# Second-quarter weights loaded in halves, block-diagonal states copied in two steps, one product split between two engines: a fused attention and maxout kernel on one core

## The chip, the cores and the metric

The kernel runs on one core of a Trainium2 chip. The metric is the time of one execution on the device in microseconds (us), and the figure used is the median of several executions. One execution was also recorded by the hardware profiler. Its *span* runs from the first to the last recorded instruction; its own time is longer, because launch and completion lie around the span.

The engines are named as in the profile: PE (TensorE matrix multiplies), PEld (its weight loads), DVE (VectorE), ACT (ScalarE), POOL (GpSimd) and SP (SyncE, here the queue that issues nearly all DMAs).

## The reference

Two stages are fused. The first is an attention between a sequence `x` (8 batches, 8 heads, 512 rows, 64 columns) and a small `state` (32 rows per head). It goes both ways: the sequence reads the state and the state reads the sequence. The second is a maxout layer over the 512 joined head columns.

```python
scores = scale * np.matmul(x, state.transpose(0, 1, 3, 2))
a = np.exp(scores - scores.max(-1, keepdims=True))
a /= a.sum(-1, keepdims=True) + 1e-09
xread = np.matmul(a, state)
...
sread = np.matmul(a2, x)            # the same with the roles exchanged
y = np.concatenate([xread, sread], axis=2)
x = y.transpose(0, 2, 1, 3).reshape(B * S, H * D)   # 4352 rows of 512
h1 = x @ w1                          # w1, w2: 512 x 1024
h2 = x @ w2
g = np.maximum(h1, h2)
out = g @ w_out                      # w_out: 1024 x 512
```

## The kernel before, in words

The maximum is written as `max(h1, h2) = relu(h1 - h2) + h2`. So the kernel needs `wd = w1 - w2` (512 x 1024) for the relu branch and `wwo = w2 @ w_out` (512 x 512) for the linear branch. It makes both on the chip, in bf16, from weights that arrive in four quarters of 256 columns of the 1024 (`FQ = 256`, `q` = 0 to 3). Per quarter there are three tensors: `w2f[q]`, `w1f[q]`, `wof[q]`, 512 KB each in f32. `w2_cast` makes the bf16 copy `w2b`, `w2_tr_mm`/`w2_tr_ev` transpose it on PE and copy it to `w2t`, `w_sub` subtracts to `wd`, `wo_cast` makes the bf16 `wo`, and `w_wo_mm` multiplies `w2t` by `wo` (L559; two matmuls for each of the four row blocks `i`, one for each half `f` of the quarter). `w_wo_ev` adds the rounds up in `w2acc`.

For each batch `b` the attention weights `a` (128 rows, four row blocks `c`, two head groups `g`) are transposed into `AT[b]`. The state is multiplied with `wd` and `wwo` beforehand: `sw_mm` makes `SW[b]`. Then `l1_mm` (L433) multiplies `SW[b]` by `AT[b]` for each of eight column blocks `f`, `l1_ev` applies the relu and writes `R[b]`. `l2` (or `l2_open`, L445, and `l2_part`, L449) makes the 512 output columns of one row block in a PSUM bank, and `l2_out` copies them to `OB[b]`, which `store` writes out.

The states stand in the tile `sbd` in block-diagonal form: `sbd[64 j : 64 j + 64, b, k, 32 j : 32 j + 32]`, with `j` = 0, 1. Batches 0 and 1 are brought in by themselves (`load_state`, `state_mm`, `state_ev`). Batches 2 to 7 are loaded together (`load_states`), cast on POOL (`states_cast`), transposed by one DMA into the tile `stt` (`states_dma`, L161), and copied from there into `sbd` by `states_ev(j, eng)`: one copy for each `j`, with 64 partitions and 768 elements.

The order of the work is written out by hand. Each engine runs its instructions in the order of the program text (`manual_schedule`), and waits by semaphores are put in where data or buffers need them. The text has two parts:

* L587 to L855: the loads in order, all weight preparation, the whole of batch 0, and batch 1 up to the end of its first layer. PSUM has two pools of four banks, `ps` and `pa`, handed out in turn. `idle` puts in matmuls on zeros.
* L858 on: the loop over `b` = 1 to 7. For `b` = 1 it begins with the scores and the normalisation of batch 2 (`norm` has its product on POOL) and goes on to batch 1's second layer in four row blocks `c`. After `c` = 1 it puts in `sw_all(2)`.

The loads of SP carry eight semaphores that are used in turn. In the built program the issue of a load therefore waits until the load eight places before it has landed. A load into a buffer that is still read waits for its last reader too: `load_w2(3)` waits for `w_sub(0)` on POOL.

Three places matter for the change. First, the product `norm_mul_pair(0, 2, "P")` at L668 on POOL, behind which POOL has, in this order, `wo_cast_h(0)`, `w1_cast_h(1)`, `wo_cast_h(1)`, `w_sub(0)`, `w2_cast(1)` and `wo_cast(1)` (L716). Next to it DVE has `norm_mul_pair(0, 3, "V")`. Second, L714 to L722, where DVE has `w_sub(1)` and `w2_tr_ev(1)`, and PE then `w_wo_mm(1, 1)`. Third, L829 to L852, where `states_ev(1, "A")` and `states_ev(0, "V")` stand ahead of the eight relu evictions of batch 1 on ACT and DVE; these free the banks that the transposes `sread_tr_mm` (L353) and the scores of batch 2 (L271) take.

Of the kernel before, what the change touches and what calls it, by code (L numbers as in the profile page):

```python
# [8 lines left out]
F32 = mybir.dt.float32  # L9
# [6 lines left out]
def kernel(  # L16
# [9 lines left out]
    nc = tc.nc  # L26
    B, H, S, D = x.shape
    _, _, Ns, _ = state.shape
    L = S + Ns
    DM = H * D  # L30
    FF = moe_w1.shape[1]
    NC = S // 128
    NF = FF // 128
    NQ = 4
    FQ = FF // NQ
# [5 lines left out]
    stage = ctx.enter_context(tc.tile_pool(name="stage", bufs=1))  # L41
# [5 lines left out]
    pa = ctx.enter_context(tc.tile_pool(name="pa", bufs=4, space=bass.MemoryType.PSUM))  # L47
    ctx.enter_context(tc.manual_schedule())

    def bank(dtype=F32, pool=None):  # L50
        n = 512 if dtype == F32 else 1024
        if pool is pa:
            return pa.tile([128, n], dtype, tag="acc", name="acc")
        return ps.tile([128, n], dtype, tag="ps", name="ps")

    def copy(eng, o, i):
        if eng == "A":
            nc.scalar.copy(o, i)  # L58
        elif eng == "V":
            nc.vector.tensor_copy(o, i)  # L60
        else:
            nc.gpsimd.tensor_copy(o, i)  # L62
# [5 lines left out]
    sbd = consts.tile([128, B, 4, 2 * Ns], BF16, name="sbd")  # L68
    wd = consts.tile([128, 4, FF], BF16, name="wd")
    wwo = consts.tile([128, 4, DM], BF16, name="wwo")  # L70
    wo = consts.tile([128, NF, DM], BF16, name="wo")
# [11 lines left out]
    xf_t, st = {}, {}  # L83
# [12 lines left out]
    w2f, w1f, wof, w2b = {}, {}, {}, {}  # L96

    def load_w2(q, second=False):
        wf, w, tag = (w1f, moe_w1, "w1f") if second else (w2f, moe_w2, "w2f")
        wf[q] = stage.tile([128, 4, FQ], F32, tag=tag, bufs=3, name=tag)  # L100
        nc.sync.dma_start(out=wf[q], in_=w[:, q * FQ:(q + 1) * FQ].rearrange("(i p) f -> p i f", p=128))

    def load_w1(q):
        load_w2(q, True)

    def load_wo(q):
        wof[q] = stage.tile([128, 2, DM], F32, tag="wof", bufs=3, name="wof")
        nc.sync.dma_start(out=wof[q], in_=moe_w_out[q * FQ:(q + 1) * FQ, :].rearrange("(f p) n -> p f n", p=128))
# [15 lines left out]
    P = {}  # L124
# [35 lines left out]
        P["st"] = xio.tile([128, NC * 256], BF16, tag="xb", name="stt")  # L160
        nc.sync.dma_start_transpose(out=P["st"].rearrange("p (m r) -> p m r", m=8), in_=sbr.rearrange("p m j d -> p (m j d)"))  # L161

    def states_ev(j, eng):
        o = sbd[64 * j:64 * j + 64, 2:B, :, 32 * j:32 * j + 32].rearrange("p b k (l m) -> p (b k) l m", l=4)
        copy(eng, o, P["st"][64 * j:64 * j + 64, :].rearrange("p (m k l) -> p k l m", m=8, l=4)[:, 8:])


    def cast_half(b, g, eng):
# [19 lines left out]
    def cast_pair(b, k, eng, m=1):  # L188
        xo = st[b]["xo"]
        for j in range(k, k + m):  # L190
            copy(eng, xo[:, :, j, 2:130].rearrange("p c (i d) -> p i c d", i=2),
                 xf_t[b][:, 2 * j:2 * j + 2, :].rearrange("p i (c d) -> p i c d", c=NC))

    def xt_pair_mm(b, k, pool=None):
        d = st[b]
        if "xt" not in d:
            d["xt"] = at.tile([128, NC, 4, 128], BF16, tag="xt", name="xt")
        p = P["xt", k] = bank(BF16, pool)
        for c in range(NC):
            nc.tensor.transpose(p[:, c * 128:(c + 1) * 128], d["xo"][:, c, k, 2:130], ident)  # L200

    def xt_pair_ev(b, k, eng):
        copy(eng, st[b]["xt"][:, :, k, :], P["xt", k][:, 0:512].rearrange("p (c t) -> p c t", c=NC))

    def att_tiles(b):
        d = st[b]
        d["e"] = at.tile([128, 2, NC, 4, Ns], BF16, tag="e", name="e")
        d["a"] = at.tile([128, 2, NC, 4, Ns], BF16, tag="a", name="a")
        d["es"] = at.tile([128, 2, 2 * NC, 2], F32, tag="es", name="es")
        d["er"] = at.tile([128, 2, 2 * NC, 2], F32, tag="er", name="er")  # L210

    def scores_pair_mm(b, k, pool):
        d = st[b]
        if "e" not in d:
            att_tiles(b)
        p = P["sc", k] = bank(F32, pool)
        for c in range(NC):
            nc.tensor.matmul(p[:, c * 64:c * 64 + 64], d["xt"][:, c, k, :], sbd[:, b, k, :],
                             start=(c == 0), stop=(c == NC - 1))
# [5 lines left out]
    def reduce_pair(b, k):  # L225
        d = st[b]
        nc.vector.tensor_reduce(d["es"][:, k // 2, :, k % 2], d["e"].rearrange("p g c i n -> p (g c) i n")[:, :, k, :],
                                axis=mybir.AxisListType.X, op=ALU.add)
# [65 lines left out]
        (nc.gpsimd if eng == "P" else nc.vector).tensor_mul(  # L294
            av, ev, d["er"][:, hh].unsqueeze(3).to_broadcast([128, 2 * NC, 2, Ns]))

    def norm_mul_pair(b, k, eng):
        d = st[b]
        ev = d["e"].rearrange("p g c i n -> p (g c) i n")[:, :, k, :]
        av = d["a"].rearrange("p g c i n -> p (g c) i n")[:, :, k, :]  # L300
        (nc.gpsimd if eng == "P" else nc.vector).tensor_mul(
            av, ev, d["er"][:, k // 2, :, k % 2].unsqueeze(2).to_broadcast([128, 2 * NC, Ns]))

    def norm(b, hh, eng, sums=True):
        norm_sums(b, hh, sums)
# [137 lines left out]
    def l2_open(b, c, p, start, stop):  # L443
        for g in range(2):
            nc.tensor.matmul(p, AT[b][:, g, c, :], SW[b][:, g, FF:WC], start=(start and g == 0), stop=(stop and g == 1))  # L445

    def l2_f(b, c, p, fs, start, stop):
        for j, f in enumerate(fs):
            nc.tensor.matmul(p, R[b][:, f, c * 128:(c + 1) * 128], wo[:, f, :],  # L449
                             start=(start and j == 0), stop=(stop and j == len(fs) - 1))  # L450

    def l2_out(b, c, p, eng):
        if b not in OB:
            OB[b] = big.tile([128, NC, DM], F32, tag="ob", name="ob")
        copy(eng, OB[b][:, c, :], p)

    def l2(b, c):
        p = bank(F32, pa)
        l2_open(b, c, p, True, False)
        l2_f(b, c, p, range(NF), False, True)  # L460
        l2_out(b, c, p, "A" if c % 2 else "V")
# [59 lines left out]
    def wo_cast_h(j, eng):  # L521
        copy(eng, wo[:, j, :], wof[0][:, j, :])
# [23 lines left out]
    def w_sub(q, i0, i1, eng):  # L546
        (nc.gpsimd if eng == "P" else nc.vector).tensor_sub(  # L547
            wd[:, i0:i1, q * FQ:(q + 1) * FQ], w1f[q][:, i0:i1], w2f[q][:, i0:i1])

    def wo_cast(q, eng):  # L550
        copy(eng, wo[:, 2 * q:2 * q + 2, :], wof[q])

    ROUNDS = [[0], [1], [2], [3]]

    def w_wo_mm(r, i, pool=None):
        p = P["wwo", r, i] = bank(F32, pool)
        fs = [f for q in ROUNDS[r] for f in (2 * q, 2 * q + 1)]
        for f in fs:
# [7 lines left out]
    def w_wo_ev(r, i, eng):  # L566
        if r == 0:
            copy(eng, w2acc[:, i, :], P["wwo", r, i])
        else:
            nc.vector.tensor_tensor(wwo[:, i, :] if r == len(ROUNDS) - 1 else w2acc[:, i, :], P["wwo", r, i],  # L570
                                    w2acc[:, i, :], op=ALU.add)
# [3 lines left out]
    def idle(n, cols=256):  # L575
        if idle_p[0] is None:
            idle_p[0] = bank(F32, pa)
        for j in range(n):
            nc.tensor.matmul(idle_p[0][:, 0:cols], wz[:, 0:128], wz[:, 0:cols], start=True, stop=True)  # L579
# [17 lines left out]
    load_h(1, 0)  # L597
    load_state(1, nc.sync)
    load_w2(1)
    load_w1(1)  # L600
    load_wo(1)
    load_w2(2)
    load_w1(2)
    load_w2(3)
# [31 lines left out]
    scores_pair_mm(0, 0, pa)  # L636
    idle(1)
    cast_pair(0, 3, "V")
    xt_pair_mm(0, 2)
    xt_pair_ev(0, 2, "V")  # L640
    state0_neg("P")
    scores_pair_ev(0, 0)
    reduce_pair(0, 0)
    scores_pair_mm(0, 1, pa)
    scores_pair_ev(0, 1)
    reduce_pair(0, 1)
    w2_cast_h(0, "P")
# [17 lines left out]
    sw_h_mm(0, pa)  # L665
    reduce_pair(0, 3)
    norm_sums(0, 1, False)
    norm_mul_pair(0, 2, "P")  # L668
    norm_mul_pair(0, 3, "V")
    wo_cast_h(0, "P")  # L670
    w1_cast_h(1, "P")
    w2_tr_h_ev(0, "A")
# [38 lines left out]
    sw_ev(1, 0, FQ, 0, "A")  # L711
    l2_part(0, 0)
    w2_tr_mm(1)
    w_sub(1, 0, 4, "V")  # L714
    w2_tr_ev(1, "V")
    wo_cast(1, "P")  # L716
    sw_two_mm(1)
    sw_two_ev(1, 1, "V")
    w_wo_ev(0, 0, "A")
# [106 lines left out]
    l2_open(0, 0, ACC[0], False, True)  # L826
    l2_open(0, 1, ACC[1], False, True)
    l2_out(0, 1, ACC[1], "A")
    states_ev(1, "A")  # L829
    l2_out(0, 0, ACC[0], "V")  # L830
    states_ev(0, "V")
    l1_mm(1, 6, pa)
    cast_half(3, 1, "P")
    l1_ev(1, 6, "A")
# [23 lines left out]
    for b in range(1, B):  # L858
        n = b + 1
        if b + 2 < B:  # L860
            if b > 1:
                cast_x(b + 2, ("P", "P"))
                xt_dma(b + 2)
        for f in range(NF if b > 1 else 0):
            l1(b, f)
        if n < B:
            for hh in range(2):
                scores(n, hh)
            for hh in range(2):
                norm(n, hh, "P")  # L870
            at_dma(n)
            if b + 2 < B:
                cast_xo(b + 2)
            if b + 3 < B:
                load_x(b + 3)
        else:
            moe_sread()
        for c in range(NC):
            if b == B - 1 and c == NC - 1:
                l2_last(b, c)  # L880
            else:
                l2(b, c)
            if n < B:
                if c == 1:
                    sw_all(n)
                    sread_mm(n, pa)
                if c == 2:
                    sread_norm(n)
                if c == 3:
                    sread_tr(n, "A")  # L890
            elif c < NC - 1:
                store(b, c, c + 1)
        if n < B:
            store(b)
# [30 lines left out]
```

## Time and profile before

| what | us |
|---|---|
| median of five executions | 148.01 |
| lowest and highest of the five | 147.92 and 149.12 |
| the profiled execution's own time | 148.33 |
| its span | 146.5 |
| PE busy in the span | 140.0 |
| DVE, ACT, POOL busy in the span | 84.0, 70.2, 59.5 |

The granted TensorE clock was 0.995 of full speed over the span. A busy PE is not a PE at its peak, because matmuls are pipelined and their ends are modelled; but where PE's starts follow each other at their least distance, nothing but PE's own work can shorten the stretch. A matmul of 512 columns takes 0.38 us in the profile, and the next one starts 0.216 us after it (16 of L433 take 3.45 us in the chain of waits). PE has 3.68 us of busy time in the first 5 us and 3.78 us in the next 5. The DMA engines moved between 283 and 375 GB/s from about 3.4 to 34.9 us.

### The profile page before, as it was taken

How to read it: one execution, taken by the hardware profiler on the slowest of the kernel's cores; microseconds unless marked ns; L12 is line 12 of the kernel's file. 1: busy time of each engine (PE TensorE's matmuls, PEld its weight loads, DVE VectorE, ACT ScalarE, POOL GpSimd, SP SyncE). 2: the span in 40 equal slices, each digit the busy share in tenths (PEclk: the TensorE clock that was granted, in tenths of full speed). 3: DMA queues.
4: the chain of work that ended last, by engine and by line, in shares of the span. 5: the costliest groups of instructions: out<-in, count | busy, mean ns of one | idle time of the engine just before them, and what ended most of it. 6: DMA issues, size and time to landing. Idle time of an engine off the chain costs nothing.

```text
span 146.5 us, 3213 instructions
## 1 busy us (share of the span) xinstructions
PE 140.0 (96%) x1300; PEld 69.8 (48%) x1300; DVE 84.0 (57%) x173; ACT 70.2 (48%) x135; POOL 59.5 (41%) x81
## 2 busy tenths in 40 slices
PE   6879999999999999999999999999999999999990
PEld 4455444364544445444544444454445344754460
DVE  3484685879786648464854585376557464621110
ACT  4367757786791546236440735171537145511110
POOL 2359644866946522925291447146500500000000
PEclk9999999999999999999999999999999999999998
DMA  4999999999739999498948784877306032402422
GB/s 117 317 325 351 356 361 363 361 350 197 151 63 323 152 349 291 96 169 321 257 85 258 285 183 76 282 293 144 72 2 286 7 72 107 179 4 72 143 111 104
DMA packets 37695, 29.44 MB, mean 201 GB/s; under 512 B 21296, under 2 KB 34864, under 8 KB 36784
## 3 DMA queue, kind: packets, MB, share of 16 engines
q1 hardware_dynamic: 37408, 29.17, 70.0%
q8 instruction: 10, 0.16, 0.5%
q10 hardware_dynamic: 272, 0.07, 0.2%
q14 instruction: 5, 0.04, 0.1%
HBM read 15.34 MB, written 8.91 MB: 165 GB/s over the span
## 4 chain that ended last, share of the span: by engine, by line
PE 83%; POOL 5%; DMA 4%; ACT 3%; issue 1%; DVE 1%; SPq 1%; POOLq 0%; ACTq 0%
PE acc L449 35%; PE ps L433 16%; PE acc L445 10%; PE ps L559 4%; DMA xf<-in_x_dram 4%; PE ps L368 3%; PE ps L489 2%; PE acc L499 2%; PE ps L271 2%; POOL wd L547 2%; POOL wo L62 2%; PE acc L335 1%; PE acc L473 1%; PE acc L497 1%; ACT r L422 1%
## 5 line engine op out<-in xcount | busy, mean ns | idle before, releaser
L449 PE MATMUL acc<-wo,r 128*128 128x512 bf16 x248 | 59.6, 380 | 0.0
L449 PEld LDWEIGHTS <-r 128*128 128x128 bf16 x248 | 23.8, 98 | 28.8 <-issue 0.6
L58 ACT COPY ob<-acc 128x512 f32<-128x512 f32 (+2 forms) x17 | 9.4, 554 | 49.1 <-PE acc L449 27.7
L433 PE MATMUL ps<-aT,sw 128*128 128x512 bf16 x118 | 27.9, 380 | 0.0
L424 DVE TENSOR_SCALAR r<-ps 128x512 bf16<-128x512 f32 x26 | 18.0, 691 | 14.3 <-PE ps L433 14.2
L294 POOL TENSOR_TENSOR a<-e,er 128x512 bf16<-128x512 bf16 x14 | 14.4, 1048 | 26.0 <-ACT e L276 18.8
L422 ACT ACTIVATE r<-ps 128x512 bf16<-128x512 f32 x33 | 19.6, 602 | 6.1 <-PE ps L433 5.5
L62 POOL CAST xb<-xf 128x1024 bf16<-128x1024 f32 x12 | 13.5, 1128 | 16.9 <-DMA xf<-in_x_dram 16.9
L60 DVE COPY ob<-acc 128x512 f32<-128x512 f32 (+1 forms) x17 | 10.9, 644 | 16.3 <-PE acc L449 14.6
L433 PEld LDWEIGHTS <-sw 128*128 128x128 bf16 x128 | 12.2, 98 | 13.7
L62 POOL CAST xo<-xf 128x512 bf16<-128x512 f32 x28 | 16.1, 615 | 5.4 <-DMA xf<-in_x_dram 5.0
L445 PE MATMUL acc<-sw,aT 128*128 128x512 bf16 x62 | 18.2, 381 | 0.0
L60 DVE CAST sw<-ps 128x512 bf16<-128x512 f32 x15 | 9.8, 686 | 11.0 <-PE ps L368 10.6
L58 ACT CAST sw<-ps 128x512 bf16<-128x512 f32 (+1 forms) x21 | 11.0, 574 | 2.9 <-PE ps L368 1.5
L287 DVE TENSOR_REDUCE es<-e 128x16 f32<-128x512 bf16 x14 | 9.2, 656 | 1.8 <-ACT e L276 1.8
L276 ACT ACTIVATE e<-ps 128x512 bf16<-128x512 f32 x14 | 7.8, 604 | 0.8 <-PE ps L271 0.2
L579 PE MATMUL acc<-wz 128*128 128x256 bf16 x32 | 6.6, 343 | 1.2 <-DVE ones L617 1.2
L445 PEld LDWEIGHTS <-aT 128*128 128x128 bf16 x62 | 5.0, 98 | 4.4
L559 PE MATMUL ps<-wo,w2t 128*128 128x512 bf16 x24 | 6.7, 379 | 0.1
L570 DVE TENSOR_TENSOR w2acc<-ps,w2acc 128x512 f32<-128x512 f32 x8 | 5.2, 687 | 1.8 <-PE ps L559 1.7
L547 POOL TENSOR_TENSOR wd<-w1f,w2f 128x1024 bf16<-128x1024 f32 x2 | 4.7, 2356 | 1.7 <-DMA w1f<-in_moe_w_dram 1.7
L271 PEld LDWEIGHTS <-xt 128*128 128x128 bf16 x112 | 4.3, 98 | 2.1 <-issue 0.5
(109 smaller groups left out, 145.3 us busy)
## 6 DMA issues: line engine op xcount, KB each, us to landing
xf<-in_x_dram SPq DMA_DIRECT2D x14, 512.0 KB, 5.0
out_dram<-ob SPq DMA_DIRECT2D x7, 1024.0 KB, 4.2
w2f<-in_moe_w_dram SPq DMA_DIRECT2D x3, 512.0 KB, 6.8
w1f<-in_moe_w_dram SPq DMA_DIRECT2D x3, 512.0 KB, 8.7
wof<-in_moe_w_out_dram SPq DMA_DIRECT2D x3, 512.0 KB, 8.0
xf<-in_x_dram SPq DMA_DIRECT2D x4, 256.0 KB, 3.9
out_dram<-ob SPq DMA_DIRECT2D x3, 256.0 KB, 2.0
w2f<-in_moe_w_dram SPq DMA_DIRECT2D x2, 256.0 KB, 6.1
```

Of the source, the lines that this page charges most:

```text
L58: nc.scalar.copy(o, i)
L60: nc.vector.tensor_copy(o, i)
L62: nc.gpsimd.tensor_copy(o, i)
L276: nc.scalar.activation(out=ev.rearrange("p (g c) i n -> p g c (i n)", g=2), in_=P["sc", hh].rearrange("p (c g m) -> p g c m", c=NC, g=2), ...
L287: nc.vector.tensor_reduce(d["es"][:, hh], ev, axis=mybir.AxisListType.X, op=ALU.add)
L294: (nc.gpsimd if eng == "P" else nc.vector).tensor_mul(av, ev, d["er"][:, hh].unsqueeze(3).to_broadcast([128, 2 * NC, 2, Ns]))
L422: nc.scalar.activation(out=o, in_=p, func=ACTF.Relu)
L424: nc.vector.tensor_scalar(o, p, scalar1=0.0, scalar2=None, op0=ALU.max)
L433: nc.tensor.matmul(p, SW[b][:, g, f * 128:(f + 1) * 128], AT[b][:, g].rearrange("p c t -> p (c t)"), start=(g == 0), stop=(g == 1))
L445: nc.tensor.matmul(p, AT[b][:, g, c, :], SW[b][:, g, FF:WC], start=(start and g == 0), stop=(stop and g == 1))
L449: nc.tensor.matmul(p, R[b][:, f, c * 128:(c + 1) * 128], wo[:, f, :], start=(start and j == 0), stop=(stop and j == len(fs) - 1))
L559: nc.tensor.matmul(p, w2t[:, f, i, :], wo[:, f, :], start=(f == fs[0]), stop=(f == fs[-1]))
```

## The change

There are four edits. (1) `load_w1(1)` and `load_wo(1)` become two loads of 256 KB each: for W1 by row blocks (two of the four), for Wo by halves `f`. Their use is cut the same way: `w_sub(1)` on DVE in two instructions, `wo_cast(1)` on POOL in two. (2) `states_ev` gets a range of batches. Where it stood it now copies batch 2 alone (64 x 128 instead of 64 x 768 elements, on each of ACT and DVE); batches 3 to 7 (64 x 640) are copied in the loop at `b` = 1 after the first row block of the second layer. (3) The product of pair 2 of batch 0 is cut by head group: POOL makes `g` = 0, and DVE makes `g` = 1 after its own product of pair 3. (4) The scores of pair 1 of batch 0 stand ahead of the transposes of pair 2 on PE.

```diff
+    def load_w1_part(q, g):
+
+        if q not in w1f:
+            w1f[q] = stage.tile([128, 4, FQ], F32, tag="w1f", bufs=3, name="w1f")
+        nc.sync.dma_start(
+            out=w1f[q][:, 2 * g:2 * g + 2],
+            in_=moe_w1[256 * g:256 * g + 256, q * FQ:(q + 1) * FQ].rearrange("(i p) f -> p i f", p=128))
...
+    def load_wo_part(q, j):
+        if q not in wof:
+            wof[q] = stage.tile([128, 2, DM], F32, tag="wof", bufs=3, name="wof")
+        nc.sync.dma_start(out=wof[q][:, j, :], in_=moe_w_out[q * FQ + 128 * j:q * FQ + 128 * j + 128, :])
...
-    def states_ev(j, eng):
-        o = sbd[64 * j:64 * j + 64, 2:B, :, 32 * j:32 * j + 32].rearrange("p b k (l m) -> p (b k) l m", l=4)
-        copy(eng, o, P["st"][64 * j:64 * j + 64, :].rearrange("p (m k l) -> p k l m", m=8, l=4)[:, 8:])
+    def states_ev(j, b0, b1, eng):
+        o = sbd[64 * j:64 * j + 64, b0:b1, :, 32 * j:32 * j + 32].rearrange("p b k (l m) -> p (b k) l m", l=4)
+        copy(eng, o, P["st"][64 * j:64 * j + 64, :].rearrange("p (m k l) -> p k l m", m=8, l=4)[:, 4 * b0:4 * b1])
...
-    def norm_mul_pair(b, k, eng):
+    def norm_mul_pair(b, k, eng, g0=0, g1=2):
...
+    def wo_cast_part(q, j, eng):
+        copy(eng, wo[:, 2 * q + j, :], wof[q][:, j, :])
...
-    load_w1(1)
-    load_wo(1)
+    load_w1_part(1, 0)
+    load_w1_part(1, 1)
+    load_wo_part(1, 0)
+    load_wo_part(1, 1)
...
+    scores_pair_mm(0, 1, pa)
     xt_pair_mm(0, 2)
     xt_pair_ev(0, 2, "V")
     state0_neg("P")
     scores_pair_ev(0, 0)
     reduce_pair(0, 0)
-    scores_pair_mm(0, 1, pa)
...
-    norm_mul_pair(0, 2, "P")
+    norm_mul_pair(0, 2, "P", 0, 1)
     norm_mul_pair(0, 3, "V")
+    norm_mul_pair(0, 2, "V", 1, 2)
...
-    w_sub(1, 0, 4, "V")
+    w_sub(1, 0, 2, "V")
+    w_sub(1, 2, 4, "V")
     w2_tr_ev(1, "V")
-    wo_cast(1, "P")
+    wo_cast_part(1, 0, "P")
+    wo_cast_part(1, 1, "P")
...
-    states_ev(1, "A")
+    states_ev(1, 2, 3, "A")
     l2_out(0, 0, ACC[0], "V")
-    states_ev(0, "V")
+    states_ev(0, 2, 3, "V")
...
             else:
                 l2(b, c)
+            if b == 1 and c == 0:
+                states_ev(1, 3, B, "A")
+                states_ev(0, 3, B, "V")
```

## The prediction

> **What bounds the kernel now.** I read the busy time by stage first, since the share over the span mixes stages. The columns are the stage, its length, then busy time and instructions of PE, PEld, DVE, ACT and POOL, the clock, the DMA share and GB/s.
>
> ```profile
> 15.00:18.86 3.86, 3.69 (x44) 1.64 (x43) 2.78 (x5) 3.09 (x7) 2.43 (x3) 1.00 1.09 354
> 18.86:25.00 6.14, 6.14 (x55) 3.15 (x55) 4.72 (x7) 3.46 (x6) 2.08 (x2) 1.00 1.09 367
> ...
> 36.00:38.60 2.60, 2.60 (x49) 1.50 (x42) 1.57 (x7) 1.75 (x3) 2.54 (x5) 1.00 0.42 89
> 38.60:42.42 3.82, 3.48 (x17) 1.57 (x16) 3.82 (x7) 3.76 (x6) 3.47 (x4) 1.00 0.63 120
> 42.42:47.00 4.58, 4.58 (x36) 2.38 (x36) 3.08 (x8) 1.91 (x4) 1.94 (x2) 1.00 0.88 231
> ```
>
> PE fills its stages from 18.86 on, except 38.60 to 42.42, where DVE and ACT are the full ones. So I took the chain of waits next (start, length, what).
>
> ```profile
> 10.63 0.79 POOL a L301
> 11.42 0.55 POOL wo L62
> ...
> 17.76 1.05 POOL wo L62
> 18.81 0.04 issue
> 18.86 1.02 PE ps L559 x4
> ...
> 38.61 0.58 ACT ob L58
> 39.20 0.01 issue
> 39.21 0.02 ACTq L422
> 39.23 1.55 ACT sbd L58
> 40.78 0.02 issue
> 40.80 1.58 ACT r L422 x3
> 42.38 0.04 issue
> 42.42 0.22 PE acc L353
> ```
>
> It shows three regimes: up to 18.86 POOL's queue sets the pace, from 18.86 to 38.6 and from 42.4 to the end PE's own work does, and between them ACT. From 42.4 on every piece is PE's, so a microsecond won before 42.4 stays won if no later load or buffer is late. The change touches the first and the third regime only. Last I read the timelines around each edit; their rows are named as they are used, and these carry most:
>
> ```profile
> 10.52 0.42 DVE L301 TENSOR_TENSOR a<-e,er 128x256 bf16<-128x256 bf16 x1
> 10.63 0.79 POOL L301 TENSOR_TENSOR a<-e,er 128x256 bf16<-128x256 bf16 x1 [0.25 <-DVE er L288]
> ```
>
> **The states (edit 2), the larger term.** PE starts the first layer of batch 1 at 38.41 and the scores of batch 2 at 42.48: 4.07 us. Its work in between is 16 matmuls at 0.216 (3.45) and two transposes at 0.056 (0.11), together 3.56. The lost 0.51 is one wait: the second transpose at L353 takes the bank that ACT's third relu (L422) frees at 42.38, and that relu is late because ACT's copy of 1.55 stands before all of them. In the change this copy has 128 instead of 768 elements. The nearest rows are ACT's 64x128 copies of batch 1's state (0.26) and this copy itself; with 0.2 us fixed and the rest by elements, (1.55 - 0.2)/6 + 0.2 = 0.43. I take 0.43. Its start does not move: stt was issued at 31.82 and landed 7.4 later, at 39.2, behind a DMA stream that the change leaves where it is. So ACT copies from 39.22 to 39.65, and three relus at a start-to-start distance of 0.49 free the bank at about 41.2. PE, back to back, asks for it at 41.98 if the stage begins as now, at 41.5 if it begins 0.5 earlier. Both are later than 41.2, so the wait is gone: **-0.51**. It would be smaller only if ACT's copy took over 1 us. On DVE the copy of 1.28 shrinks too; its relus then begin before 40.6 instead of at 41.09, and PE doesn't wait for them now.
>
> Next in line behind this wait is the transposed x of batch 2: issued at 37.03, median landing 4.4 later, 41.4. PE would want it at 42.48 - 0.51 = 41.97 or, with the first term below, at 41.7. A margin of 0.3.
>
> The removed elements return as copies of 640: ACT about 0.2 + 1.35 x 640/768 = 1.33, DVE 1.28 x 640/768 = 1.07. ACT's stands between the exp of batch 2 (ends 44.33) and the eviction of row block 1 (wanted when PE ends it, 47.42): idle cover of 3.1, enough for 1.33. DVE's stands between the eviction of row block 0 (ends 46.30) and the first eviction of SW[2] (its matmuls begin at 47.42). A cover of 1.1 or a little more for 1.07; if POOL holds it up, DVE is late by up to 1 us. Behind it on DVE wait the evictions of SW[2]; PE reads SW[2] only at L433 at 53.04, and the next bank that it needs from them is the fourth row block's, at 50.8. So 3 us of slack, price nothing. On SP nothing is queued for these copies; the tile stt keeps its buffer 6 us longer, and its next user is a cast in the following iteration, after 53.
>
> **The split loads (edit 1).** POOL's cast of Wo begins at 17.76, when the load has landed (its completion stands at 17.71 in the trace), and ends at 18.80; PE's L559 starts at 18.86. What is late next: PE's own queue is ready about 18.57 (its last matmul of L449 starts at 18.35) and DVE's copy to w2t runs 17.89 to 18.58. So the most that a faster cast gives here is 18.86 - 18.63 = 0.23. The 512 KB loads follow each other at about 1.45 us (512 KB at 354 GB/s is 1.48), so the first half of Wo lands some 0.73 before 17.71, at 17.0, and the first half of W1 at about 15.5. The casts of halves take 0.61 each on POOL (L62 at 11.92), 0.55 start to start. Were POOL free, both would be done by 18.37. It may not be: DVE's subtraction of W1 (1.23, now two of about 0.62) and POOL's casts disturb each other. These two rows show how:
>
> ```profile
> 35.23 0.87 DVE L294 TENSOR_TENSOR a<-e,er 128x512 bf16<-128x512 bf16 x1
> ...
> 35.50 1.50 POOL L62 CAST xb<-xf 128x1024 bf16<-128x1024 f32 x1
> ```
>
> POOL's product before (34.51 + 1.05) ends at 35.56, and DVE's ends 0.54 after that, at 36.10; POOL's cast, 1.04 when alone (17.76), ends 0.90 after DVE's. They take turns. So DVE's first half, ready at 16.08, waits for POOL's w2b cast to end at 16.39; the second runs to about 17.6; POOL's first half cast then runs to 18.15 and its second to 18.7. L559 takes the second half for its second matmul alone, at 18.85. Either way w2t at 18.58 decides: **-0.22**. Bounds: 0 if the half lands no earlier than the whole, -0.23 if all is free. If POOL went first, DVE's second half and the copy to w2t would end 0.3 later, +0.1.
>
> In cost, SP issues two more loads (0.43 to 0.68 each here). The second-quarter issues wait for the load eight places before them, and those completions stand at 11.60 and 12.36, so w2f(2) goes out at about 11.6 instead of 10.45, w1f(2) at 12.4 instead of 10.97. Both land at 19 and 21 behind a stream that has no gap, 7 us later: hidden. The next, w2f(3), waits for POOL at 15.40 in either kernel. The rows of 256 KB loads with the same row length, sfr, give 0.7 us each, no dearer than half of 1.45. A page speaks against this edit. The Trainium skill, page "DMA: Bandwidth & Descriptors", under "Bandwidth", tells one to batch transfers to 1 MiB or more for 75% of peak. By that rule halving would cost stream time; here the stream runs at 354 GB/s on loads of 256 and 512 KB. By the rule the first term would be near 0, by the rows it is -0.22.
>
> **The shared product (edit 3).** POOL's half would take 0.40 by elements (0.79/2), and POOL's queue would end 0.39 earlier. But the 0.79 is itself a taken turn: DVE's product ends at 10.94, POOL's 0.48 after that, at 11.42; alone a 512-element product takes 1.05 (9.33), so 256 take 0.52. With two products on DVE, POOL has its half (0.26) after DVE's first, to 11.20, and DVE's second runs then, to about 11.38, ahead of POOL's cast. So POOL's cast ends at about 11.93 instead of 11.97: -0.05. Bounds: +0.05 if DVE runs both first, -0.22 if they don't meet, since then ACT's cast of w2b (11.62 + 0.62) and its aT copy (to 12.73) bind PE's L433 at 12.83 instead of 13.05. The PE stream from 13.05 to 18.12, and w2t with it, follows this step, so it adds to the term above: **-0.05**.
>
> The Trainium skill, "SBUF — State Buffer", under "Who interferes with whom", says that a DVE instruction with two SBUF inputs and a POOL instruction that reads SBUF share a port pair as an exclusive lock, and that the later one fully blocks. The rows above agree (0.54 and 0.90 after the other's end). By the lock the step is worth -0.05, without it -0.22.
>
> **The moved scores (edit 4).** Scores of pair 1 start at about 6.5 instead of 6.80. Their reductions on DVE stand behind a cast that waits until 7.48 for x; so nothing moves. The delayed transposes of pair 2 (6.57, then 6.7) are evicted at 7.82 behind that same cast. **0**; if that cover were gone, -0.3 at most.
>
> **Sum.** -0.51 - 0.22 - 0.05 = -0.78. Does the head's 0.27 survive to 38.4? PE's stream from 18.86 is back to back, and the loads that feed it land at fixed times: w2b(2) is cast by 20.42 (used at 20.80), wd(3) by 27.51 (28.09), wo(2) by 24.28 (24.94), the last x casts by 30.05 (30.84). The least margin is 0.38, above 0.27. Against the profiled execution's 148.33 the sum is 147.55. That execution lies 0.32 over the median of five; the sum takes work out of the span (146.5 to 145.7) and nothing from the 1.83 around it, so I put it on the median: 148.01 - 0.78 = 147.23, forecast **147.2**.
>
> **Rivals.** (A) *The head's gain is hidden anyway.* The half of Wo waits behind DVE's subtraction and its second half lands as late as before, or the transposed x at 41.4 sets the scores. For it: 17.76 is a landing, and the margin at 41.4 is 0.3. Against it: the row at w2t. Then only the states count: 148.01 - 0.51 = 147.5. (B) *No turns.* The halves don't meet; edits 1 and 3 give 0.23 + 0.22, with the states 0.96: 147.05. Against it: the rows at 35.23 and 35.50. (C) *The load stream becomes late; slower.* Place: SP's issues of w2f(2) and w1f(2), 1.2 to 1.4 later. If the stream lost s there, every weight quarter and x would land s later; PE absorbs 0.4 by the margins and loses the rest, and stt lands late too. The states' 0.51 is repaid at s = 0.91; at the full s = 1.4 the time is 148.01 + 1.0 - 0.5 = 148.5. Against it: both loads now land 8 us after issue, in a queue, so 7 would do. (D) *The change doesn't do what it says*: ACT's copy of 128 elements costs nearly as much as that of 768, and the wait stays. With the head alone 147.75. Against it: 0.26 for 64x128.
>
> **How the numbers follow.** Chances: the forecast 0.54, A 0.22, B 0.12, D 0.06, C 0.06. The range runs from B with room for the scatter of a median (five executions lay 147.92 to 149.12, the four lower ones within 0.4) to D: 146.8 to 147.9. That leaves out C and little else. A measurement here can tell 0.5%, or 0.74 us, from no change. The forecast's -0.78 lies just past it: somewhat over half of it counts as faster, nearly all of B, a small part of A. So faster 0.48, same 0.46, slower 0.06.
>
> **What would show it.** After the change ACT's copy at 39.2 is about 0.43 long and no wait of PE remains between 38 and 42.4. L559 starts near 18.6, released by w2t on DVE. POOL's half product is followed at about 11.4 by its cast, not at 11.0. From the scores of batch 2 to the end, every start lies 0.78 earlier. It is wrong if xt's landing releases the scores, or if POOL's cast still releases L559, or if weight loads land later than now.

## The result and the profile after

| | before | after |
|---|---|---|
| median, us (executions) | 148.29 (76) | 147.5 (39) |
| ratio, 95% interval | | 0.9941 (0.9925 to 0.9957) |
| span of the profiled execution, us | 146.5 | 145.2 |

The change made the kernel 0.6% faster: 0.0059 x 148.29 = 0.87 us, by the interval 0.64 to 1.11. The forecast was 0.78. The ratio leaves out executions more than 1.5% above the fastest of their kernel (four of the 39), so it is not the quotient of the two medians.

In the answers below, the line numbers of the changed kernel are higher (L433 is now L447, L422 is L436, L445 and L449 are L459 and L463, L559 is L576, L271 is L284, L353 is L367, L301 is L315). First the busy time by stage, in the same columns as before the change.

```profile
15.00:18.59 3.59, 3.54 (x42) 1.50 (x41) 3.17 (x6) 2.61 (x6) 2.27 (x3) 1.00 1.09 353
18.59:25.00 6.41, 6.41 (x57) 3.30 (x56) 4.63 (x8) 4.15 (x7) 2.28 (x3) 1.00 1.08 365
36.00:38.30 2.30, 2.30 (x18) 1.32 (x17) 1.28 (x7) 1.54 (x3) 2.24 (x6) 1.00 0.94 122
38.30:41.40 3.10, 3.10 (x21) 1.49 (x19) 3.10 (x6) 2.71 (x7) 2.53 (x3) 1.00 0.61 130
41.40:46.00 4.60, 4.60 (x37) 2.22 (x34) 4.04 (x9) 2.84 (x4) 2.25 (x4) 1.00 0.94 256
```

PE now fills the stage from 38.30 to 41.40 too; before, it had 3.48 us of 3.82 there. The chain of waits over the same stretch shows that ACT has left it:

```profile
37.03 0.86 PE acc L459 x4
37.89 0.43 PE acc L447 x2
...
40.91 0.43 PE ps L447 x2
41.34 0.11 PE acc L367 x2
41.46 0.47 PE ps L284 x16
```

Before, ACT's copy and three of its relus stood between L445 and L353. Now the two transposes of L367 follow the first layer with no wait. ACT's timeline shows why, and when the copy begins:

```profile
37.93 0.59 ACT L58 COPY ob<-acc 128x512 f32<-128x512 f32 x1 [0.50 <-PE acc L459]
38.88 0.41 ACT L58 COPY sbd<-stt 64x128 bf16<-64x128 bf16 x1 [0.36 <-DMA stt<-sbr]
39.31 0.60 ACT L436 ACTIVATE r<-acc 128x512 bf16<-128x512 f32 x1
...
42.98 1.29 ACT L58 COPY sbd<-stt 64x640 bf16<-64x640 bf16 x1
46.28 0.59 ACT L58 COPY ob<-acc 128x512 f32<-128x512 f32 x1 [2.01 <-PE acc L463]
```

The copy waits for a landing (the bracket: 0.36 us idle, ended by the DMA into stt), takes 0.41, and the relus begin at 39.31 instead of 40.80. The rest of the states lies in the loop and ends 2.01 us before ACT is wanted.

To compare executions, whose loads land at different times, I cut each trace at three program points: DVE's second reciprocal of batch 0, the first matmul of `w2t` by `wo` in round 1, and the first scores matmul of batch 2. From the first to the second is the *head*, from the second to the third the *body*. Behind it every trace has 100.32 us to the last matmul.

| | reciprocal at | head | body |
|---|---|---|---|
| before | 10.23 | 8.62 | 23.62 |
| after | 9.91 | 8.25 | 23.14 |

So in these two executions the head gave 0.37 and the body 0.48, 0.85 together, near the measured 0.87. What the head gives depends on when loads land, as the experiments show. The spans differ by 1.3, because in the changed kernel's profiled execution the reciprocal came 0.32 earlier by an earlier landing of x (6.91 against 7.45), and its end was 0.13 shorter. (The expectations of the first experiments count the head from DVE's product instead, 0.29 later: 8.34 and 7.96.)

### The profile page after: what moved, and what is told of

The parts are those of the page before. It is cut to its first block, busy times and chain, and to the rows that moved or that the text cites. A ratio compares the mean times of both kernels' runs of the same rounds, so it can differ in the third digit from the quotient of the medians.

```text
span 145.2 us, 3221 instructions
## 1 busy us (share of the span) xinstructions
PE 139.3 (96%) x1300; PEld 69.6 (48%) x1300; DVE 85.8 (59%) x176; ACT 70.3 (48%) x136; POOL 59.4 (41%) x82
## 4 chain that ended last, share of the span: by engine, by line
PE 92%; DMA 3%; SPq 1%; DVE 1%; ACT 1%; issue 1%
PE acc L463 37%; PE ps L447 18%; PE acc L459 10%; PE ps L576 4%; DMA xf<-in_x_dram 3%; PE ps L382 3%; PE ps L503 2%; PE acc L513 2%; PE ps L284 2%; PE acc L349 2%; PE acc L447 1%; PE acc L487 1%; PE acc L511 1%; SPq L91 1%; PE ps L554 1%; PE acc L596 1%
## 5 line engine op out<-in xcount | busy, mean ns | idle before, releaser
L463 PE MATMUL acc<-wo,r 128*128 128x512 bf16 x248 | 59.6, 380 | 0.0
L463 PEld LDWEIGHTS <-r 128*128 128x128 bf16 x248 | 23.8, 98 | 28.7 <-issue 0.6
L447 PE MATMUL ps<-aT,sw 128*128 128x512 bf16 x118 | 27.9, 379 | 0.0
L436 ACT ACTIVATE r<-ps 128x512 bf16<-128x512 f32 x33 | 19.7, 601 | 5.5 <-PE ps L447 5.0
L62 POOL CAST xb<-xf 128x1024 bf16<-128x1024 f32 x12 | 12.9, 1082 | 16.0 <-DMA xf<-in_x_dram 15.6
L447 PEld LDWEIGHTS <-sw 128*128 128x128 bf16 x128 | 12.2, 98 | 13.7
L459 PE MATMUL acc<-sw,aT 128*128 128x512 bf16 x62 | 18.2, 381 | 0.0
L459 PEld LDWEIGHTS <-aT 128*128 128x128 bf16 x62 | 5.0, 98 | 4.4
L576 PE MATMUL ps<-wo,w2t 128*128 128x512 bf16 x24 | 6.7, 380 | 0.0
L62 POOL CAST w2b<-w2f 128x1024 bf16<-128x1024 f32 (+1 forms) x4 | 3.7, 930 | 3.4 <-DMA w2f<-in_moe_w_dram 3.4
```

Source lines behind the costliest of these rows:

```text
L436: nc.scalar.activation(out=o, in_=p, func=ACTF.Relu)
L447: nc.tensor.matmul(p, SW[b][:, g, f * 128:(f + 1) * 128], AT[b][:, g].rearrange("p c t -> p (c t)"), start=(g == 0), stop=(g == 1))
L576: nc.tensor.matmul(p, w2t[:, f, i, :], wo[:, f, :], start=(f == fs[0]), stop=(f == fs[-1]))
```

## The experiments

All are timed against the kernel before on the same chip. An interval of one experiment is about 0.3% to either side, so the single edits are read from the traces, and the ratios only say whether they speak against it.

| kernel | ratio (95%) | head | body |
|---|---|---|---|
| edit 2 alone | 0.9974 (0.9943 to 1.0006) | 8.40 | 23.14 |
| edit 2, ACT's part alone | 0.9941 (0.9915 to 0.9968) | 8.78 | 23.14 |
| edit 2, DVE's part alone | 0.9984 (0.9956 to 1.0012) | 8.71 | 23.65 |
| edit 1 alone | 1.0010 (0.9977 to 1.0043) | 8.40 | 24.29 |
| edit 3 alone | 0.9996 (0.9965 to 1.0026) | not read | not read |
| edits 1 and 3 | 0.9976 (0.9946 to 1.0007) | 8.37 | 24.53 |
| edits 1 and 2 | 0.9937 (0.9907 to 0.9968) | 8.60 | 23.48 |
| all but edit 4 | 0.9945 (0.9912 to 0.9979) | 8.27 | 23.31 |
| the changed kernel again | 0.9902 (0.9866 to 0.9938) | 9.09 | 23.13 |
| the changed kernel, more idle matmuls | 0.9932 (0.9903 to 0.9960) | 8.25 | 23.13 |

Two more kernels were executed once each: the kernel before again (head 8.40, body 23.62) and a kernel without one DVE product.

### The states, whole and in halves

```diff
# edit 2 alone, on the kernel before
-    states_ev(1, "A")
+    states_ev(1, 2, 3, "A")
     l2_out(0, 0, ACC[0], "V")
-    states_ev(0, "V")
+    states_ev(0, 2, 3, "V")
...
+            if b == 1 and c == 0:
+                states_ev(1, 3, B, "A")
+                states_ev(0, 3, B, "V")
# ACT's part alone: the second copy stays (0, 2, B, "V") at the old place; DVE's part alone: the first stays (1, 2, B, "A")
```

> Edit 2 alone on the kernel before: the copies at the old place cover batch 2, batches 3 to 7 are copied in the loop. Two stretches are read in each trace: the head, from the start of DVE's product of pair 3 to the first matmul of w2t by wo in round 1 (before 8.34 us, after 7.96), and the body, from there to the first scores matmul of batch 2 (before 23.63, after 23.14). Theory: head as before (8.34), body 23.14, ACT's copy at the old place about 0.43 us, time 0.5 us under the kernel before (ratio 0.9965). Rival (the whole gain comes from the head): body 23.63, ratio 1.000.

> Half of edit 2 on the kernel before: only ACT's copy at the old place is cut to batch 2 and its rest moved to the loop; DVE copies all its 768 elements at the old place. Theory (ACT's relus free the bank that PE waits for): body 23.14 us as with all of edit 2, ratio 0.9965. Rival (DVE's relus matter as much): body between 23.4 and 23.63, ratio 0.998 to 1.000.

> The other half: only DVE's copy is cut, ACT copies all its 768 elements at the old place. Theory: body 23.63 us as before, ratio 1.000, and the bank is freed by ACT's third relu as before. Rival: body 23.14 to 23.4, ratio 0.9965 to 0.998.

The body is 23.14 with all of edit 2, 23.14 with ACT's part and 23.65 with DVE's part. (The head with edit 2 alone was expected as before, 8.62, and is 8.40; the account of the split loads below says why.) With ACT's part alone the chain of waits is PE's from end to end, though DVE's copy of 768 still stands in its old place:

```profile
41.75 0.86 PE acc L433 x4
42.62 0.43 PE ps L433 x2
43.05 0.11 PE acc L353 x2
43.16 0.47 PE ps L271 x16
```

With DVE's part alone it is ACT's as before, and it begins with the landing of the states, 0.02 us after the end of ACT's eviction before the copy (38.73):

```profile
31.52 7.24 DMA stt<-sbr
38.75 0.02 issue
38.78 1.56 ACT sbd L58
40.34 0.02 issue
40.35 1.58 ACT r L422 x3
41.94 0.04 issue
41.98 0.22 PE acc L353
```

So the whole 0.48 is ACT's copy in front of the relus that free the bank; DVE's copy cost nothing. The interval of ACT's part alone excludes 1; the ratio of all of edit 2 agrees with the expected 0.9965 but can't be told from 1.

### The loads, and the loads with the product

```diff
# edit 1 alone, on the kernel before
-    load_w1(1)
-    load_wo(1)
+    load_w1_part(1, 0)
+    load_w1_part(1, 1)
+    load_wo_part(1, 0)
+    load_wo_part(1, 1)
...
-    w_sub(1, 0, 4, "V")
+    w_sub(1, 0, 2, "V")
+    w_sub(1, 2, 4, "V")
...
-    wo_cast(1, "P")
+    wo_cast_part(1, 0, "P")
+    wo_cast_part(1, 1, "P")
# edits 1 and 3: also the split product
```

> Edit 1 alone on the kernel before: W1 and Wo of the second quarter in two loads each, their subtraction and cast in two each. Theory: head 8.11 (8.34 - 0.22), released by DVE's copy to w2t and not by POOL's cast, body 23.63, ratio 0.9985. Rival (POOL's half casts wait behind DVE's subtraction until nothing is won): head 8.34. Rival (the load stream becomes later by two more issues): the loads behind land later, head over 8.34 and body over 23.63.

> Edits 1 and 3 on the kernel before, without edit 2. Theory (the head's gain is given back where the states are copied, since the load of the transposed states lands at a time that the head doesn't move, and ACT's copy of 768 and three relus follow it): head 8.25 instead of 8.62 us after DVE's second reciprocal, body longer than 23.63 by as much, about 24.0, ACT's copy released by the landing; ratio 1.000. Rival (the head's gain stays, whatever edit 2 does): body 23.63, ratio 0.9975.

With the loads alone the head fell from 8.62 to 8.40, by the predicted 0.22, and PE's matmul at 18.35 follows DVE's copy to w2t (17.60 to 18.29). One row each of the timelines of POOL, DVE and PE:

```profile
17.27 1.29 POOL L62 CAST wo<-wof 128x512 bf16<-128x512 f32 x2 [1.07 <-DMA wof<-in_moe_w_out_dram]
17.60 0.69 DVE L60 COPY w2t<-ps 128x1024 bf16<-128x1024 bf16 x1 [0.25 <-PE ps L553]
18.35 0.86 PE L575 MATMUL ps<-wo,w2t 128*128 128x512 bf16 x3
```

But the body grew by 0.67. A longer body was expected only if the load stream became later, and then with a longer head. The chain of waits shows why it grew:

```profile
32.22 7.16 DMA stt<-sbr
39.38 0.02 issue
39.40 1.53 ACT sbd L58
40.94 0.01 issue
40.95 1.58 ACT r L435 x3
42.54 0.04 issue
42.58 0.22 PE acc L366
```

ACT stood idle for 0.53 us until the landing of the transposed states. From there on copy, relus and bank take their fixed time. The second run was made to test just this; there the copy again starts at a landing (38.93). Its head is 8.37 and its body 24.53, where 8.25 and about 24.0 were expected. About 0.3 of that body lies at its start: PE's second matmul at L576 comes 0.51 after the first instead of 0.22, since POOL's cast of the second half of Wo ends only at 18.12. Counted from the start of ACT's whole copy, the scores begin 3.26 us later before the change (39.22 to 42.48), 3.24 with edit 1 (39.40 to 42.64), 3.24 with edits 1 and 3 (38.96 to 42.20) and 3.26 with DVE's part of edit 2 (38.78 to 42.04). While the whole copy stands there and ACT waits for the landing, nothing that shortens the head can move the scores. So the loss is shown for these two profiled executions. The ratios don't settle it for the median: 0.9976 for edits 1 and 3 is what the rival said (0.9975), and its interval holds the theory's 1.000 too. In other executions the head ends so late that ACT comes after the landing and the gain can stay: in the repeated kernel before, stt had landed at 38.28 and ACT copied at 40.02. How many executions are of which kind is open.

```diff
# edits 1 and 2
+ edit 1 as above, edit 2 as above
```

> Edits 1 and 2 on the kernel before. Theory: with the states' copies out of the way the head's gain stays: head 8.40 us (8.62 before), body 23.14, ratio 0.995 (-0.71 us). Rival (the head's gain is hidden in any case): as the states alone, ratio 0.9965.

The ratio 0.9937 is as expected for both edits; but its interval holds the rival's 0.9965 too. In its profiled execution the reciprocal came at 9.31, 0.9 us earlier than before, and the fixed landings showed again: POOL's casts of Wo had to wait until 16.96 and ended at 18.28, so PE's second matmul at L575 came 0.43 after the first instead of 0.22. The head was 8.60, set by PE's own work and DVE's copy to w2t (17.16 to 17.85), and the body 23.48; 8.40 and 23.14 were expected. The scores began at 41.39 in it, at 41.29 in the changed kernel and at 41.26 without edit 4, from reciprocals at 9.31, 9.91 and 9.68. In the first of these the transposed x of batch 2 had landed at 41.35, just ahead of the scores: this is the next wait in line, as the prediction had it.

### The shared product and the turns of DVE and POOL

```diff
# edit 3 alone, on the kernel before
-    norm_mul_pair(0, 2, "P")
+    norm_mul_pair(0, 2, "P", 0, 1)
     norm_mul_pair(0, 3, "V")
+    norm_mul_pair(0, 2, "V", 1, 2)
# the kernel before without DVE's product
-    norm_mul_pair(0, 3, "V")
+    nc.vector.memset(st[0]["a"].rearrange("p g c i n -> p (g c) i n")[:, :, 3, :], 0.0)
```

> Edit 3 alone on the kernel before: POOL makes half of the product of pair 2, DVE the other half. Theory: POOL's next cast ends some 0.15 us earlier after the start of DVE's product (1.30 instead of 1.46), the first layer's first matmul of batch 0 too, but the head stays at 8.34, since the landing of the whole of Wo releases POOL's cast there; ratio 1.000. Rival (the product's queue on POOL sets the head by itself): head 8.19, ratio 0.999.

> The kernel before with DVE's product of pair 3 of batch 0 left out: DVE writes zeros there, and reads nothing. Theory (POOL's product waits for the end of DVE's, which reads the same memory): POOL's product of 256 elements takes 0.52 us instead of 0.79 and starts at the same distance behind the reciprocal. Rival (a 256-element product costs POOL 0.79 by itself): 0.79 again.

The profiled execution of edit 3 alone took 151.22 us, 2.8 over the median of that kernel, so its head and body are not read; only the distances on POOL are, which agree in all traces. From DVE's reciprocal to the end of POOL's next cast it takes 1.74 us before, 1.59 with edit 3 alone and in the changed kernel, and 1.57 without DVE's product. The ratio of 0.9996 agrees with no gain from this edit alone, as expected. POOL's timeline in the kernel without DVE's product:

```profile
10.97 0.62 POOL L301 TENSOR_TENSOR a<-e,er 128x256 bf16<-128x256 bf16 x1 [0.25 <-DVE a L669]
```

The same instruction took 0.79 beside DVE's product and 0.62 without it: neither the 0.52 that I had scaled from 512 elements nor the rival's 0.79. So DVE's turn cost POOL 0.17. In the changed kernel the turns show on both engines, DVE's two products first (one row, x2), then POOL's half and its cast:

```profile
10.20 0.83 DVE L315 TENSOR_TENSOR a<-e,er 128x256 bf16<-128x256 bf16 x2
```

```profile
10.31 0.57 POOL L315 TENSOR_TENSOR a<-e,er 128x128 bf16<-128x128 bf16 x1 [0.26 <-DVE er L301]
10.83 0.67 POOL L62 CAST wo<-wof 128x512 bf16<-128x512 f32 x1
11.45 0.61 POOL L62 CAST w1b<-w1f 128x512 bf16<-128x512 f32 x1
```

DVE's first product ends at 10.62, POOL's half at 10.88, DVE's second at 11.03, and POOL's cast 0.47 after that. The Trainium skill, "SBUF — State Buffer", section "Who interferes with whom", calls this an exclusive lock between a DVE instruction with two SBUF inputs and a POOL instruction that reads SBUF. These rows agree, and they add that the two take it in turn.

### The moved scores, the repetitions, and idle matmuls

```diff
# all but edit 4, on the changed kernel
-    scores_pair_mm(0, 1, pa)
     xt_pair_mm(0, 2)
...
     reduce_pair(0, 0)
+    scores_pair_mm(0, 1, pa)
# more idle matmuls, on the changed kernel
     scores_pair_mm(0, 0, pa)
-    idle(1)
+    idle(3)
...
     w2_cast_h(0, "P")
-    idle(1)
+    idle(7)
     xt_pair_mm(0, 3)
```

> The changed kernel without edit 4: the scores of pair 1 stand behind the transposes of pair 2 again. Theory: the swap is worth nothing, so head 8.25, body 23.14 and a ratio to the changed kernel of 1.000 within the interval. Rival: the swap is worth up to 0.3 us, then DVE's second reciprocal comes later after the landing of the last quarter of x than in the changed kernel (3.0 us there, 2.8 in the kernel before).

> The kernel before once more, for the scatter of the two stretches between executions: head 8.34 and body 23.63 within 0.1 us if they are set by the program, more if DMA landings scatter them. The landing of the last quarter of batch 0's x, 7.45 in the first profile and 6.91 in the changed kernel's, should scatter by some 0.5 us whatever the kernel; the rival is that the change made it earlier, then it is 7.45 again.

> The changed kernel once more, beside the next three on one chip. Head 8.25 us from DVE's second reciprocal to the first matmul of w2t by wo in round 1, body 23.14 us from there to the scores of batch 2; ratio 0.994.

> The changed kernel with 8 more matmuls on zeros where PE waits for batch 0's x (2 behind the scores of pair 0, 6 ahead of the transposes of pair 3). Theory (in some executions the granted clock falls to half for 3.41 us at about 7 to 12 us, since PE does little work while it waits, and that costs about 1.2 us): the fall becomes rare, and the median is 0.2 us or more under the changed kernel's. Rival (the fall doesn't depend on work in that wait, or the added matmuls delay the transposes of pair 3): as many falls as before, or the reciprocal later, and a median not under the changed kernel's.

Without edit 4 the ratio is 0.9945, and 0.9902 for the changed kernel beside it, with overlapping intervals. The reciprocal came 2.83 us after the landing of x, against 3.00 in the changed kernel and 2.78 to 2.99 in the other traces without edit 4 in which the clock stayed full, so no gain of the swap shows, and what there is of a difference goes the other way. It is not settled whether that is the swap: in the changed kernel's trace DVE's cast of x took 0.65, in the two of the kernel before 0.43 and 0.60.

The landing of x scatters as expected: 7.45 and 7.56 in the two traces of the kernel before, 6.91 and 7.88 in the two of the changed kernel. The early landing of 6.91 was no effect of the change. The repeated kernel before kept its body (23.62) but not its head: 8.40 against 8.62, where 0.1 was allowed. In the profiled execution of the repeated changed kernel PE was granted half of its clock from 8.93 to 12.34, past the reciprocal at 11.05; its head of 9.09 shows that and not the edits, and its body is 23.13. The idle matmuls brought no gain that can be measured (147.6 against 147.25 for the changed kernel beside them); in their trace the reciprocal came 3.28 after the landing of x, which the rival had named.

## Why the prediction was right, step by step

**The states.** Predicted -0.51, measured -0.48, by the mechanism that was named: ACT's copy, and not DVE's. The copy of 128 elements was predicted at 0.43 and took 0.41, that of 640 at 1.33 and took 1.29. That its start would not move was right in part: it moved from 39.22 to 38.88, because the landing did, from 39.18 to 38.85. In the kernel before, ACT's eviction ended at 39.20, so ACT and the landing came together there. That the landing can hold this start mattered more than the prediction made of it. The returned copies were hidden, but closely on DVE: predicted at 1.07, measured at 1.50. It ran beside POOL's two products and ended 0.58 after them. That it waited for POOL, as the prediction feared, fits these rows (of DVE and of POOL), but no run tests it.

```profile
44.83 1.50 DVE L60 COPY sbd<-stt 64x640 bf16<-64x640 bf16 x1
46.64 1.29 DVE L60 CAST sw<-ps 128x512 bf16<-128x512 f32 x2 [0.31 <-PE ps L382]
...
43.69 2.06 POOL L307 TENSOR_TENSOR a<-e,er 128x512 bf16<-128x512 bf16 x2 [2.86 <-DVE er L301]
```

The copy ends at 46.33 and the next eviction waits for PE, so 0.31 of its cover was left.

**The split loads.** Predicted -0.22, released by w2t; measured -0.22 in the trace of edit 1 alone. The turns were as described: POOL's first half cast, issued at 16.73 in the changed kernel, ran into DVE's second subtraction (to 17.05), and the two casts took 1.36 together instead of 1.16 (0.55 to the second's start and 0.61).

```profile
15.63 1.42 DVE L561 TENSOR_TENSOR wd<-w1f,w2f 128x512 bf16<-128x512 f32 x2
17.41 0.69 DVE L60 COPY w2t<-ps 128x1024 bf16<-128x1024 bf16 x1 [0.35 <-PE ps L554]
```

The stream did not become later: its last load ahead of the transposes, x of batch 3, landed between 36.34 and 36.91 in the seven traces of kernels with whole loads, and between 36.44 and 36.96 in the seven with split ones. But the term has a condition that the prediction left out: it is there only where the landing of Wo is the last thing. In the repeated kernel before, and with edit 2 alone, the head is 8.40 without it, since PE was later and the load not: the reciprocal came at 11.24 and 11.37 and Wo landed at 17.27 and 17.29, against 10.23 and 17.71 in the first trace. So the edit gives 0.22 in one execution and nothing in another. Nor does w2t alone decide: with the reciprocal as early as 9.30 and 9.31, POOL's second half cast held up PE's second matmul by 0.2 to 0.3.

**The shared product.** Predicted -0.05, measured -0.15 (1.74 to 1.59, and the head from 8.40 with edit 1 alone to 8.25 with all four). This term was mis-sized. The order of the turns and the end of POOL's half were right (0.68 after the start of DVE's first product, predicted and measured). But DVE's second product took less time than assumed, and POOL's cast, waiting for its turn, ended 0.47 after it and not 0.55. The bound of -0.22 had it inside. The sign that the prediction gave, a cast 0.88 after the start of DVE's first product, did not show: the cast is recorded from 0.63 after it, and its wait as 0.67 instead of 0.60.

**The moved scores.** Predicted 0; one trace without it shows no gain.

**The sum.** -0.22 - 0.15 - 0.48 = -0.85, against -0.78 predicted and -0.87 measured (0.64 to 1.11). That the three lie so close is partly luck. Against the repeated kernel before the head gave 0.15 and not 0.37, and the measured ratio mixes both kinds of execution. Adding the terms holds for the four edits together; for edit 1 by itself it fails in its trace, which gives 0.22 in the head and loses more in the body. Rival A had the right mechanism (a landing that the head can't move), but the place was the copy of the states, and edit 2 takes that away. Rival B's 0.96 lies inside the interval; it has the rows of POOL's and DVE's turns against it. Against C stand the landings of x of batch 3, against D the copy of 0.41.

## What to carry to other kernels

Look for the landings that no edit moves, and see which work hangs on each: a gain ahead of such a point can be worth nothing until the work behind it has been cut. A copy for later batches that stands ahead of evictions on an in-order engine costs what the freed banks come late; moving the part that isn't needed yet costs nothing while its new place has idle time. Two engines that take turns at the same memory share a product less well than their element counts say, but better than not at all.

## What the runs showed of the hardware

In some executions the granted TensorE clock fell to half for one stretch of 3.41 us near the start. The stages of the repeated kernel before (columns as above; the clock is the third number from the end):

```profile
4.00:7.40 3.40, 1.64 (x18) 0.83 (x16) 1.48 (x4) 1.20 (x4) 0.48 (x1) 1.00 1.01 302
7.40:10.80 3.40, 3.21 (x31) 2.82 (x32) 2.36 (x7) 1.69 (x5) 2.68 (x4) 0.50 1.14 325
10.80:14.20 3.40, 3.23 (x88) 2.21 (x88) 1.71 (x5) 2.62 (x7) 2.56 (x5) 1.00 1.11 345
```

The same program, in its first profile, had 2.73 us of busy PE from 4.00 to 7.40 and a clock of 1.00 throughout; here it had 1.64, and the next 3.4 us were granted at half. The reciprocal came at 11.24 instead of 10.23. The Trainium skill, "TensorE: Matmul & The Clock Gate", Part 1, states a free-running activity window of 3413 ns; the length agrees with the 3.41 here. Eight more matmuls on zeros in the wait for x did not remove the fall: it was there in 2 of 12 executions of that kernel, against 11 of 40 of the changed one (those with a granted clock of 0.989 or less over the span), and the median did not improve. Whether a better placed filling would is open.

The fourteen traces show what goes ahead of the fall. I take the 3.41 us after each trace's first record of a full clock (from 3.98 in the repeated kernel before, from 5.26 in its first profile). In the five traces with the fall, which begins at the end of this stretch, PE was busy for 1.52 to 1.74 us of it; in the nine without, for 2.21 to 2.84 us. The fall does not make the difference between the two kernels: it stands in 21 of the 87 executions of the kernel before that were timed beside the experiments, about as often as in the changed one, and without it the medians are 148.2 (66) and 147.16 (29).

The transposing DMA into stt took 5.9 to 7.4 us from issue to landing in the fourteen traces, and it landed after the last load that was issued before it in each: 2.4 to 2.5 us after it in the nine traces without the fall of the clock (36.72 and 39.18 in the first, 36.44 and 38.85 in the changed kernel), 1.0 to 1.9 us in the five with it (36.34 and 38.28 in the repeated kernel before). So its landing goes with the loads ahead of it; what sets the rest of the time is open.
